# Moving the gather of an expert's sixth pair of rows from the third fixed unit to the first unit behind the branch

## The chip, the cores and the metric

The kernel runs on one core of one Trainium2 chip. The metric is the device time of one execution in microseconds (us); lower is better. Before the change three runs took 1734.55 to 1735.56 us, median 1735.2. The engines are called PE (TensorE, matrix products), ACT (ScalarE), DVE (VectorE), POOL (GpSimd) and SP (SyncE, which issues transfers). Each works through its own queue of instructions in order and waits for the others by semaphores.

## The reference

An attention without softmax makes the rows, then a mixture of eight experts works on some of them:

```python
# u, v: (8, 2496, 256), z: (8, 2496, 64); x becomes (19968, 256)
scores = z @ z.T / 2496
x = u * (maximum(scores, 0) ** 2 @ v)
do_compute = x @ w_skip > 0            # the other rows pass unchanged
e = argmax(x @ w_gate)                 # one expert of 8 for each row, with its gate
y = gate * (maximum(x @ w1[e], 0) @ w2[e])    # w1: 256 x 1024, w2: 1024 x 256
out = x + y
```

With the reference's inputs (seed 0) 10,022 of the 19,968 rows go to an expert: 1191, 1245, 1235, 1194, 1290, 1073, 1292 and 1502 to experts 0 to 7.

## The kernel before

The attention fills the first 1245 us or so. It writes the rows x to a DRAM tensor `xr` and, as each block of rows is routed, each row's number and gate to a list `lst` of its expert. Matrix products run in fp32r with a high and a low part, three products for one (`w1h`, `w1l`, `xh`, `xl`, `hh`, `hl`).

The expert stage goes through the experts in order. A **pair** is 256 rows of one expert, two tiles of 128 rows. Before a pair can be used it is gathered by `fetch` (L633): DVE copies its 256 row numbers into a small tile `go` (L637), then POOL issues two indirect DMAs (L639), each of which brings 128 rows of 1 KB from `xr`. Then `turn_pe` (L649) transposes the rows: PE turns four 128 x 128 blocks (L657), ACT takes the high part out of PSUM (L659), DVE the low part (L660). Tiles of gathered rows are called `xgf` for pairs 0 to 2 and `xgu` for later ones.

`unit` (L662) does the work on up to 512 rows. Its parts are hidden blocks `h_part` (PE L691, ACT L696 for `hh`, DVE L697 for `hl`) and pieces of the second product `y_part` (PE L710). The parts follow each other in an order written out by hand, first `lead` hidden blocks, then hidden blocks and second products in turn. `fills` is a table from a slot number to steps: the steps in slot k are issued right behind part k, into the queues of their engines, in the order of the program. So with `lead` 4, slot 1 lies behind the second hidden block, slot 3 behind the fourth, and in a unit of 256 rows slot 5 behind the second piece of the second product. At the end of a unit DVE forms the output rows (L739) and POOL scatters them, 128 a DMA (L742).

Each expert has three **fixed units** of one pair each (NFIX = 3), whatever its count. Behind them stands a **branch** (`tc.Switch`, L1032): a register holds how many pieces of 64 rows are left (`arm`), and each engine jumps to the code written for that number. `widths` (L977) cuts the pieces into units of up to 8: 7 or 8 pieces make one unit, 9 make 4 + 5, 12 make 8 + 4. In the counts above experts 0 to 7 take the code for 7, 8, 8, 7, 9, 5, 9 and 12 pieces.

The branch needs pairs 3, 4 and, where more than 1280 rows go to the expert, 5. In the kernel before, all three are gathered ahead of the branch for every expert (L1000; for expert 0 L1014 and L1017), one in each fixed unit, for pair 5 in the third. Behind the branch, L1045 to L1047 gather pairs 6 and later if there are any, `there` being the last pair that has been asked for. Entries of a list past its count point to a spare row, so that a gather of rows that don't exist reads that row.

In the queues around this place: DVE makes the `go` copies between the `hl` blocks. POOL, for experts after the first, also makes the low parts of the next expert's weights (L153, L159), gathers the next expert's pairs (L1004) and scatters the outputs. In the third fixed unit POOL's order is: scatters of the second unit, gather of pair 5, four subtractions of weights, gather of the next expert's pair 2, scatters of the third unit, branch. SP loads the weights (L97) into four staging tiles, each of which is free again when its subtraction is done. Transfers that are issued inside a branch come with an instruction of POOL for their semaphores (INC_SWDGE_SEM).

Of the kernel before, what the change touches and what calls it, by code (L numbers as in the profile page):

```python
# [23 lines left out]
NFIX = 3  # L24
# [20 lines left out]
def f32(ap):  # L45
    return ap.bitcast(F32)
# [3 lines left out]
def attn_moe(ctx, tc, zT, uT, v, wg, w1, w2, cst, pad, out):  # L50
# [75 lines left out]
    def load_w(e, eng):  # L126

        w1h, w1l, w2t = wts[e] = ([], [], [])
        raw = {}
        srcs = []  # L130
        for k in range(4):
            c, h = divmod(k, 2)
            srcs.append(
                w1[e, c * P : (c + 1) * P, h * 2 * D : (h + 1) * 2 * D].rearrange("p (a d) -> p a d", a=2)
            )
        for k in range(NF // 2):
            srcs.append(w2[e, :, 2 * k : 2 * k + 2, :])
        ahead = 3

        def bring(k):  # L140
            for m in range(len(raw), min(k, len(srcs))):
                raw[m] = stage_in(srcs[m])

        bring(3)

        def piece(k):
            bring(k + ahead)
            r = raw[k]
            if k < 4:
                w1h.append(vtile("w1h"))  # L150
                w1l.append(vtile("w1l"))
                nc.scalar.copy(w1h[k], r)
                eng.tensor_sub(w1l[k], r, f32(w1h[k]))  # L153
            else:
                for a in range(2):
                    t = vtile("w2t")
                    w2t.append(t)
                    nc.scalar.copy(t[:, 0, :], r[:, a, :])
                    eng.tensor_sub(t[:, 1, :], r[:, a, :], f32(t[:, 0, :]))  # L159

        return [lambda k=k: piece(k) for k in range(len(srcs))]
# [262 lines left out]
    def spare(rows64=True):  # L424

        if rows64:
            return ps_s.tile([P, 2, QC], F32, name="psm", tag="s")
        return ps_acc.tile([P, 1, QC], F32, name="psm", tag="acc")
# [201 lines left out]
    def load_ids(t, e, n):  # L630
        nc.sync.dma_start(t, lst[e * CAP : e * CAP + n * P, :].rearrange("(k p) c -> p k c", p=P))

    def fetch(ids, xg, n=2):  # L633


        go = rp.tile([P, 2, 1], I32, name="go", tag="go", bufs=4)
        nc.vector.tensor_copy(go[:, :n], ids[:, :, 0:1])  # L637
        for t in range(n):
            nc.gpsimd.indirect_dma_start(  # L639
                out=xg[:, t, :],  # L640
                out_offset=None,
                in_=xr,
                in_offset=bass.IndirectOffsetOnAxis(ap=go[:, t, 0:1], axis=0),
                bounds_check=N + P - 1,
                oob_is_err=False,
            )
        return xg

    def turn_pe(xg, xt, n=2, o=0, rows64=False):  # L649

        if rows64:
            ps = spare()[:, 0, :].rearrange("p (d q) -> p d q", d=2)
        else:
            ps = ps_acc.tile([P, 2, 2 * P], F32, name="pst", tag="acc")
        for t in range(n):
            for d in range(2):
                nc.tensor.transpose(ps[:, d, t * P : (t + 1) * P], xg[:, t, d * P : (d + 1) * P], ident)  # L657
        xh, xl = (x[:, :, o : o + n * P] for x in xt)
        nc.scalar.copy(xh, ps[:, :, : n * P])  # L659
        nc.vector.tensor_sub(xl, ps[:, :, : n * P], f32(xh))  # L660
# [193 lines left out]
    for s, (ci, p) in enumerate(steps):  # L854
        b, q0, n = chunks[ci]
        k = s % NP
# [110 lines left out]
    def ids_of(e, i, n=2):  # L967
        return idts[e][:, 2 * i : 2 * i + n, :]

    def pair(e, i):  # L970

        return xgs["f"][NFIX * (e % 2) + i] if i < NFIX else xgs["u"][i % 4]

    def turned(e, i):
        return xtf if e and i == 0 else xts[i % 2]
# [9 lines left out]
    def add(fills, *slots):  # L985
        for k, f in slots:
            fills.setdefault(k, []).append(f)

    def rows(e, i):
        return lambda: fetch(ids_of(e, i), pair(e, i))  # L990

    for e in range(E):
        more = e + 1 < E
        wq = load_w(e + 1, nc.gpsimd if e else nc.vector) if more else []
        narms = NARM + (2 if e == 0 else 1)
        for i in range(NFIX):
            fills = {}
            if e:

                add(fills, (1, rows(e, i + 3)), (3, lambda: turn_pe(pair(e, i + 1), turned(e, i + 1))))  # L1000
                if e == 1 and i == 0:
                    add(fills, (0, rows(1, 2)))
                if more:
                    add(fills, (4, rows(e + 1, i)))  # L1004
                if i == 0 and e + 2 < E:
                    add(fills, (6, lambda: load_ids(idts[e + 2], e + 2, 2 * NSTAT)))
                add(fills, *zip((1, 3, 5), wq[3 * i : 3 * i + 3]))
            elif i == 0:
                add(fills, (0, lambda: turn_pe(pair(0, 1), turned(0, 1))))
                add(fills, (1, gates), (1, logits), (1, route), (2, counts), (2, gate), (2, rows0), (2, rows1),  # L1010
                    (2, store), (4, store), (5, end_routes), (6, end_lists))
                add(fills, *zip((0, 2), left))
            elif i == 1:
                add(fills, (1, end_counts), (3, lambda: turn_pe(pair(0, 2), turned(0, 2))), (4, rows(0, 3)), (6, rows(0, 4)))  # L1014
                add(fills, *zip((1, 3, 5), wq[:3]))
            else:
                add(fills, (1, rows(1, 0)), (3, rows(0, 5)), (4, lambda: turn_pe(pair(0, 3), turned(0, 3))),  # L1017
                    (5, rows(1, 1)), (6, lambda: load_ids(idts[2], 2, 2 * NSTAT)))
                add(fills, *zip((1, 2, 3, 5, 6), wq[3:]))
            if more and i == NFIX - 1:  # L1020
                add(fills, (7, lambda: turn_pe(pair(e + 1, 0), turned(e + 1, 0))))
            if i == NFIX - 1:

                add(fills, (5, lambda: turn_pe(pair(e, NFIX + 1), turned(e, NFIX), 2, 2 * P)))
                n = nc.values_load(fin["arm"][0:1, e : e + 1], min_val=0, max_val=narms - 1)
                add(fills, (1, lambda: tc.switch_hint({g: n for g in ENGINES}, narms, label="rest%d" % e)))
            ids = ids_of(e, i) if e else idt_e[:, 2 * i : 2 * i + 2, :]
            xg = pair(e, i)
            unit(e, 4, ids, [xg[:, 0, :], xg[:, 1, :]], turned(e, i), fills)


        for arm in tc.Switch(n, narms, hint="rest%d" % e):  # L1032
            ws = widths(arm) if arm <= NARM else []
            if arm > NARM:
                for i in range(NFIX):
                    xg = fetch(ids_of(0, i), xgs["u"][i])
                    turn_pe(xg, xts[0])
                    unit(0, 4, ids_of(0, i), [xg[:, 0, :], xg[:, 1, :]], xts[0])
            end = NFIX + -(-sum(ws) // 4)
            i, there = NFIX, NFIX + 2  # L1040
            for j, hw in enumerate(ws):
                fills = {}
                after = ws[j + 1 :]
                nxt = i + -(-hw // 4)
                while there < min(i + 3, end - 1):  # L1045
                    there += 1
                    add(fills, (1, rows(e, there)))  # L1047
                if after:
                    xt = xts[(NFIX + j + 1) % 2]
                    add(fills, (3, lambda nxt=nxt, xt=xt: turn_pe(pair(e, nxt), xt)))  # L1050
                    if after[0] > 4:
                        add(fills, (5, lambda nxt=nxt, xt=xt: turn_pe(pair(e, nxt + 1), xt, 2, 2 * P)))
                w = -(-hw // 2)
                xg = [pair(e, i + t // 2)[:, t % 2, :] for t in range(w)]
                unit(e, hw, ids_of(e, i, w), xg, xts[(NFIX + j) % 2], fills, not more and not after, 3 if j else 4)
                i = nxt
            if arm >= NARM:
                ce = nc.values_load(fin["cnt"][0:1, e : e + 1], min_val=0, max_val=N)
                with tc.For_i((NSTAT if arm == NARM else NFIX) * UT, ce, UT) as tok:
                    it = op.tile([P, 2, 2], I32, name="it", tag="it")  # L1060
                    nc.sync.dma_start(
                        it, lst[bass.ds(tok + e * CAP, UT), :].rearrange("(k p) c -> p k c", p=P)
                    )
                    xg = fetch(it, xgs["u"][0])
                    turn_pe(xg, xts[0])
                    unit(e, 4, it, [xg[:, 0, :], xg[:, 1, :]], xts[0])
# [55 lines left out]
```

## Time and profile before

| | |
|---|---|
| median of three runs | 1735.2 us |
| the profiled execution's own time | 1747.1 us |
| its span, first to last instruction | 1745.1 us |
| mean granted clock of TensorE | 0.996 |
| busy: PE, DVE, ACT, POOL | 99%, 69%, 64%, 30% |
| expert stage | about 1245 to 1745 us |
| HBM read, written | 184.2 MB, 136.0 MB |

A row of the time line reads: start in us, length in us, engine, line of the kernel, operation, tiles as out<-in, shape, count, and in brackets the idle time of the engine before it with what ended it. A row of the groups reads: line, engine, operation, tiles, shape, count, then busy us and mean ns, then idle time before and what ended most of it. A row of the waits reads: who waited for whom, us in total, times, the longest. A row of stretches gives start:end, length, busy us (and instructions) of PE, PEld (weight loads), DVE, ACT and POOL, then the granted clock, the busy share of the 16 DMA engines and GB/s. "issue" stands for time in which an engine waited for nothing that the profile shows.

### The profile page before, as it was taken

The page shows a single profiled execution, that of the slowest core. Times are in us where ns is not written, and L with a number is a line of the kernel's source. Part 1 is how long each engine was busy: PE and PEld are TensorE (multiplying, and loading weights), DVE is VectorE, ACT ScalarE, POOL GpSimd, SP SyncE. Part 2 cuts the span into 40 slices and gives each one's busy share as a digit, 9 for nine tenths or more (in the row PEclk, how much of TensorE's full clock was granted, in tenths as well). Part 3 has the DMA queues.
Part 4 walks back from the last instruction along what each step waited for, and adds up shares of the span by engine and source line. Part 5 has one row for each costly group of instructions (what it writes and reads, how often), then busy time and mean ns, then how long its engine had stood idle before and what let it go on. Part 6 is the DMA issues. An engine that isn't in the chain of part 4 may idle for free.

```text
span 1745.1 us, 39255 instructions
## 1 busy us (share of the span) xinstructions
PE 1724.1 (99%) x15474; PEld 1537.9 (88%) x15474; DVE 1206.2 (69%) x1976; ACT 1112.6 (64%) x1409; POOL 520.1 (30%) x516
## 2 busy tenths in 40 slices
PE   9999999999999999999999999999989999999998
PEld 7888789988888998888889888888889999999997
DVE  6877877887887888788788878877744334443333
ACT  7877877787687778768777876877333333333321
POOL 1103213212211321231132023112446556635731
PEclk9999999999999999999999999999999999999999
DMA  5576699579858957985895799589543323322210
GB/s 179 152 203 193 151 247 281 144 211 258 236 146 243 277 147 204 272 239 146 236 262 162 207 261 254 140 225 250 149 111 84 90 83 106 100 61 86 86 42 26
DMA packets 408113, 303.29 MB, mean 174 GB/s; under 512 B 202768, under 2 KB 346001, under 8 KB 407152
## 3 DMA queue, kind: packets, MB, share of 16 engines
q1 hardware_dynamic: 393728, 276.37, 57.6%
q0 software_dynamic: 13632, 22.99, 4.7%
q8 instruction: 137, 2.24, 0.5%
q14 instruction: 184, 1.51, 0.3%
q10 hardware_dynamic: 432, 0.18, 0.0%
HBM read 184.21 MB, written 136.02 MB: 183 GB/s over the span
## 4 chain that ended last, share of the span: by engine, by line
PE 90%; DMA 3%; issue 3%; DVE 1%; ACT 1%; another core or an unknown queue 1%; POOL 1%; SPq 0%; POOLq 0%; DVEq 0%; ACTq 0%
PE acc L419 59%; PE y L710 10%; PE psh L691 10%; PE ps L302 8%; DMA out<-o,idt 2%; PE psm L491 1%; PE pst L657 1%; PE ps L285 0%; DMA kept<-rt 0%; DVE hl L697 0%; DVE al L390 0%; DMA raw<-in_v 0%; ACT ah L386 0%; DMA xgu<-xr,go 0%
## 5 line engine op out<-in xcount | busy, mean ns | idle before, releaser
L419 PE MATMUL acc<-ah,vh 64*128 64x512 f32 (+1 forms) x3120 | 643.7, 384 | 0.9 <-DVE ah L386 0.8
L419 PE MATMUL acc<-ah,vl 64*128 64x512 f32 (+1 forms) x3120 | 629.4, 383 | 0.0
L390 DVE TENSOR_TENSOR al<-r,ah 128x1024 fp32r<-128x1024 f32 (+1 forms) x400 | 479.8, 1206 | 135.2 <-ACT ah L386 114.9
L419 PE MATMUL acc<-al,vh 64*128 64x512 f32 (+1 forms) x3120 | 499.0, 383 | 0.6 <-DVE al L390 0.2
L590 POOL DMA_INDIRECT lst<-pair,dest x160 | 202.4, 1265 | 773.5 <-DVE dest L588 688.7
L386 ACT CAST ah<-r 128x1024 fp32r<-128x1024 f32 (+1 forms) x356 | 363.5, 1032 | 90.4 <-PE acc L419 41.8
L419 PEld LDWEIGHTS acc<-ah,vh 64*128 64x128 f32 x3120 | 329.3, 185 | 48.1 <-DVE ah L386 1.6
L419 PEld LDWEIGHTS acc<-ah,vl 64*128 64x128 f32 x3120 | 329.6, 185 | 41.6 <-DVE vl L122 0.3
L419 PEld LDWEIGHTS acc<-al,vh 64*128 64x128 f32 x3120 | 312.5, 184 | 51.0 <-DVE al L390 7.7
L376 ACT ACTIVATE r<-ps 128x1024 f32<-128x1024 f32 (+1 forms) x224 | 228.0, 1018 | 134.6 <-PE ps L302 116.1
L696 ACT ACTIVATE hh<-psh 128x512 fp32r<-128x512 f32 (+2 forms) x172 | 96.3, 572 | 287.6 <-PE psh L691 233.1
L377 ACT ACTIVATE r<-r 128x1024 f32<-128x1024 f32 (+1 forms) x224 | 236.3, 1055 | 7.1
L710 PE MATMUL y<-w2t,hh 128*128 128x256 f32 (+1 forms) x1328 | 235.8, 280 | 0.0
L697 DVE SCALAR_TENSOR_TENSOR hl<-psh,hh 128x512 fp32r<-128x512 f32 (+2 forms) x172 | 110.0, 655 | 151.9 <-ACT hh L696 121.3
L319 DVE STREAM_TRANSPOSE rt<-r 128x512 f32<-128x512 f32 x304 | 197.4, 688 | 10.2 <-DMA kept<-rt 9.4
L710 PEld LDWEIGHTS y<-w2t,hh 128*128 128x128 f32 (+1 forms) x1328 | 201.1, 186 | 1.8 <-issue 0.6
L691 PE MATMUL psh<-xt,w1h 128*128 128x256 f32 (+3 forms) x896 | 185.8, 304 | 8.6 <-DVE hl L697 5.9
L710 PE MATMUL y<-w2t,hl 128*128 128x256 f32 (+1 forms) x664 | 184.8, 278 | 0.8 <-DVE hl L697 0.7
L691 PEld LDWEIGHTS psh<-xt,w1h 128*128 128x128 f32 x896 | 142.4, 190 | 14.5 <-DVE hl L697 7.3
L691 PE MATMUL psh<-xt,w1l 128*128 128x256 f32 (+3 forms) x448 | 135.3, 302 | 0.0
L742 POOL DMA_INDIRECT out<-o,idt x77 | 76.5, 994 | 167.6 <-DVE o L739 132.5
L710 PEld LDWEIGHTS y<-w2t,hl 128*128 128x128 f32 (+1 forms) x664 | 123.0, 185 | 1.2 <-DVE hl L697 1.2
(197 smaller groups left out, 1750.6 us busy)
## 6 DMA issues: line engine op xcount, KB each, us to landing
kept<-rt SPq DMA_DIRECT2D x242, 256.0 KB
r<-kept SPq DMA_DIRECT2D x90, 512.0 KB
r<-kept SPq DMA_DIRECT2D x62, 448.0 KB
raw<-in_v SPq DMA_DIRECT2D x80, 256.0 KB
ut<-in_uT SPq DMA_DIRECT2D x32, 512.0 KB
xr<-xrow SPq DMA_DIRECT2D x128, 128.0 KB
out<-xr SPq DMA_DIRECT2D x32, 512.0 KB
raw<-in_w SPq DMA_DIRECT2D x64, 256.0 KB
```

The costliest lines, as they stand in the source:

```text
L302: nc.tensor.matmul(to, k[h, o : o + P], queries(ci, q, h, n), start=(m == 0), stop=(m == 2))
L319: nc.vector.transpose(t[:, :, 32 * k : 32 * k + 32].rearrange("p (k a) i -> p a k i", k=4), r[:, x, :].rearrange("p (a k i) -> p a k i", a ...
L376: nc.scalar.activation(r[:, :, :n], ps[:, :, :n], AF.Relu, scale=isc)
L377: nc.scalar.activation(r[:, :, :n], r[:, :, :n], AF.Square)
L386: (nc.scalar.copy if on_act(ci, p) else nc.vector.tensor_copy)(h_, r_)
L390: nc.vector.tensor_sub(l_, r_, f32(h_))
L419: nc.tensor.matmul(acc[t][:, :n], w[h, x, dd], a[h, x, :n], start=(first and t not in halves[:m]), stop=(last and t not in halves[m + 1 :]),)
L590: put = nc.gpsimd.indirect_dma_start(out=lst, out_offset=bass.IndirectOffsetOnAxis(ap=dest[:, t : t + 1], axis=0), in_=pair[:, t, :], in_o ...
L691: nc.tensor.matmul(ps[:, j * W : (j + 1) * W], wt[:, a, o : o + P], x[:, d, :W], start=(m == 0), stop=(m == 5),)
L696: nc.scalar.activation(hh[:, : G * W], ps[:, : G * W], AF.Relu)
L697: nc.vector.scalar_tensor_tensor(hl[:, : G * W], ps[:, : G * W], 0.0, f32(hh[:, : G * W]), op0=ALU.max, op1=ALU.subtract)
L710: nc.tensor.matmul(ys[t], h[:, tt], w2t[f][:, k, :], start=(f == 0 and m == 0 and t % share == 0), stop=(f == NF - 1 and m == 2), skip_gro ...
```

## The change

The gather of pair 5 leaves the third fixed unit, for expert 0 as for the others. Behind the branch the count of pairs already asked for now begins at 4. The first unit there gathers in slot 1 the first pair that is missing and in slot 3 the second, if there is one. So pair 5 is gathered in slot 1 of the first unit behind the branch, by the same three instructions, and only in the code for 9 pieces and more (those that reach pair 5).

```diff
-                add(fills, (1, rows(e, i + 3)), (3, lambda: turn_pe(pair(e, i + 1), turned(e, i + 1))))
+                if i < NFIX - 1:
+                    add(fills, (1, rows(e, i + 3)))
+                add(fills, (3, lambda: turn_pe(pair(e, i + 1), turned(e, i + 1))))
...
-                add(fills, (1, rows(1, 0)), (3, rows(0, 5)), (4, lambda: turn_pe(pair(0, 3), turned(0, 3))),
+                add(fills, (1, rows(1, 0)), (4, lambda: turn_pe(pair(0, 3), turned(0, 3))),
...
-            i, there = NFIX, NFIX + 2
+            i, there = NFIX, NFIX + 1
...
-                while there < min(i + 3, end - 1):
-                    there += 1
-                    add(fills, (1, rows(e, there)))
+                for k in range(1, min(i + 3, end - 1) - there + 1):
+                    add(fills, (1 + 2 * (k > 1), rows(e, there + k)))
+                there = max(there, min(i + 3, end - 1))
```

## The prediction

> **What bounds the kernel now.** I read the page first, then the waits of TensorE (PE) from the start of the expert stage at 1240 us, then the rows around the eight branches.
>
> ```profile
> PE 1724.1 (99%) x15474; PEld 1537.9 (88%) x15474; DVE 1206.2 (69%) x1976; ACT 1112.6 (64%) x1409; POOL 520.1 (30%) x516
> ```
> ```profile
> PE psh L691 <- DVE hl L697: 5.9, 4, 2.8
> PE psh L691 <- issue: 2.6, 4, 0.9
> PE y L710 <- DVE hl L697: 0.7, 1, 0.7
> PE psm L564 <- DVE pre L546: 0.5, 1, 0.5
> ```
>
> PE is the bound, and in the 505 us of the expert stage it waits 5.9 + 2.6 + 0.7 + 0.5 = 9.7 us. So whatever this change saves on another engine is worth at most a part of 9.7 us, while any wait that it puts in front of PE costs its full length. The four waits of 5.9 us all lie just behind a branch. The two longest are those of experts 0 and 5, the other two together are 5.9 - 2.78 - 1.90 = 1.2 us (experts 1 and 3):
>
> ```profile
> 1297.69 0.47 PE L691 MATMUL psh<-xt,w1h 128*128 128x448 f32 x1 [2.78 <-DVE hl L697]
> ```
> ```profile
> 1592.46 0.56 PE L691 MATMUL psh<-xt,w1h 128*128 128x320 f32 x2 [1.90 <-DVE hl L697]
> ```
>
> No PE wait on a gather stands in the list: every pair of rows is there in time today.
>
> **Which experts need a sixth pair.** With the reference's inputs (seed 0) the experts get 1191, 1245, 1235, 1194, 1290, 1073, 1292 and 1502 tokens. Behind the 768 of the three fixed units that leaves 7, 8, 8, 7, 9, 5, 9, 12 pieces of 64, which the code cuts into units of 7; 8; 8; 7; 4+5; 5; 4+5; 8+4. The trace agrees, at 32 such matmuls a unit (8 blocks of F, 2 halves of D, 2 terms):
>
> ```profile
> L691 PE MATMUL psh<-xt,w1h 128*128 128x512 f32 x96 | 30.5, 399 | 1.0 <-DVE hl L697 0.6 <-issue 0.4
> ...
> L691 PE MATMUL psh<-xt,w1h 128*128 128x320 f32 x96 | 22.1, 317 | 1.9 <-DVE hl L697 1.9
> ...
> L691 PE MATMUL psh<-xt,w1h 128*128 128x448 f32 x64 | 18.6, 371 | 3.9 <-DVE hl L697 3.4 <-issue 0.5
> ```
>
> Three units of 8 pieces, three of 5, two of 7. Only experts 4, 6 and 7 reach pair 5. So the change drops the gather in experts 0, 1, 2, 3 and 5, and moves it in three.
>
> **What is removed.** Per expert one index copy on DVE and two indirect gathers on POOL:
>
> ```profile
> L639 POOL DMA_INDIRECT xgu<-xr,go x48: 997/1016/1256, 1272.0 to 1698.8; - x48
> L637 DVE COPY go<-idt x45: 154/159/2807, 1271.5 to 1696.3; 128x2 int32<-128x2 int32 x45
> ```
> ```profile
> 1686.21 1.05 POOL L639 DMA_INDIRECT xgu<-xr,go  x1 [2.23 <-DVE go L637]
> 1687.56 1.01 POOL L639 DMA_INDIRECT xgu<-xr,go  x1 [0.30 <-issue]
> ```
>
> On POOL that is 2 x (1.02 + 0.30) = 2.6 us per expert ahead of the branch. What stood behind it there moves up by 2.6 us: four subtractions of the next expert's weights, the two gathers of its pair 2, and, as far as the results are ready, two scatters. PE waits for none of these, so as POOL time the 2.6 us are worth nothing; the 0.16 us on DVE neither, in a unit where PE does not wait for DVE. What could be worth something is traffic. DVE sits idle at each branch; these stretches run from its last output row to its first instruction behind the branch, in experts 1, 5, 6 and 7 (the columns I use are the length and, next to last, the DMA share):
>
> ```profile
> 1351.71:1354.99 3.28, 3.28 (x15) 2.44 (x13) 0.00 (x1) 1.69 (x3) 2.95 (x5) 1.00 0.71 229
> 1589.17:1591.92 2.75, 1.39 (x10) 1.13 (x8) 0.01 (x2) 0.95 (x3) 2.14 (x3) 1.00 0.73 209
> 1644.06:1645.92 1.86, 1.86 (x18) 1.86 (x18) 0.00 (x0) 0.92 (x2) 1.56 (x2) 1.00 0.15 35
> 1705.26:1706.63 1.37, 1.37 (x8) 1.09 (x7) 0.00 (x1) 0.60 (x1) 1.06 (x2) 1.00 0.01 6
> ```
>
> Busy DMA engines go with 2.8 to 3.3 us, idle ones with 1.4 to 1.9 us. Expert 6 gathers pair 5 like the others; what it lacks is the load of a next but one expert's weights. Those loads wait for the staging tiles that POOL's subtractions free. In experts 1 and 5 these are:
>
> ```profile
> 1353.22 2.81 POOL L159 TENSOR_TENSOR w2t<-raw,w2t 128x256 fp32r<-128x256 f32 x4
> ```
> ```profile
> 1585.54 2.81 POOL L159 TENSOR_TENSOR w2t<-raw,w2t 128x256 fp32r<-128x256 f32 x4
> ```
>
> In expert 5 they end at 1588.4, just ahead of the idle stretch, and would end at 1585.8, so that the loads run mostly before it (expert 3 lies alike); in expert 1 they would end at 1353.4, and the loads move into the stretch (expert 2 alike). I take -1.0 us for experts 3 and 5 together (2.75 - 1.86 = 0.9 in expert 5) and 0 for the rest. Bounds: -2.6 us (all of 1.2, the 0.43 us of expert 2 that is one of the "issue" waits, and 1.0 of expert 5's 1.90), and +1.0 us if experts 1 and 2 get later by 0.5 each.
>
> **What is added.** Behind the branch the gather is issued after the second hidden block (slot 1), and PE turns pair 5 in slot 5 of experts 4 and 6 and in slot 3 of expert 7. PE gets there today at:
>
> ```profile
> 1532.70 0.60 PE L657 MATMUL pst<-ident,xgu 128*128 128x128 f32 x4
> ```
> ```profile
> 1650.44 0.60 PE L657 MATMUL pst<-ident,xgu 128*128 128x128 f32 x4
> ```
> ```profile
> 1709.79 0.60 PE L657 MATMUL pst<-ident,xgu 128*128 128x128 f32 x4
> ```
>
> The second half of the pair is needed about 0.18 us later. When will it be there? The index copy stands on DVE behind the second `hl`:
>
> ```profile
> 1529.03 1.89 DVE L697 SCALAR_TENSOR_TENSOR hl<-psh,hh 128x512 fp32r<-128x512 f32 x3 [2.96 <-issue]
> ```
> ```profile
> 1645.92 1.89 DVE L697 SCALAR_TENSOR_TENSOR hl<-psh,hh 128x512 fp32r<-128x512 f32 x3 [1.87 <-ACT hh L696]
> ```
> ```profile
> 1706.63 0.69 DVE L697 SCALAR_TENSOR_TENSOR hl<-psh,hh 128x512 fp32r<-128x512 f32 x1 [1.37 <-ACT hh L696]
> 1707.87 0.69 DVE L697 SCALAR_TENSOR_TENSOR hl<-psh,hh 128x512 fp32r<-128x512 f32 x1 [0.54 <-issue]
> ```
>
> Three in 1.89 us are 0.60 apart, so the second ends at 1530.3, 1647.2 and 1708.6, and the copy 0.16 later. From the copy's end to the first gather this trace has 0.28 us (1282.63 + 0.16 to 1283.07) and 0.79 us (1685.26 + 0.16 to 1686.21, the row above):
>
> ```profile
> 1282.63 0.16 DVE L637 COPY go<-idt 128x2 int32<-128x2 int32 x1
> ...
> 1283.07 1.24 POOL L639 DMA_INDIRECT xgf<-xr,go  x1 [3.27 <-DVE go L637]
> ```
> ```profile
> 1685.26 0.16 DVE L637 COPY go<-idt 128x2 int32<-128x2 int32 x1
> ```
>
> The second gather starts 1.35 us after the first (above), or 1.42 us as two transfers do inside a branch:
>
> ```profile
> 1529.58 1.00 POOL L742 DMA_INDIRECT out<-o,idt  x1 [0.31 <-issue]
> 1536.84 0.98 POOL L742 DMA_INDIRECT out<-o,idt  x1 [6.25 <-DVE o L739]
> 1538.26 0.97 POOL L742 DMA_INDIRECT out<-o,idt  x1 [0.45 <-DVE hl L697]
> ```
>
> Landing is seen where two gathers run alone, those of 1686.21 and 1687.56; the DMA engines are busy with them in these two stretches and idle between them:
>
> ```profile
> 1687.90:1688.70 0.80, 0.80 (x10) 0.80 (x9) 0.40 (x1) 0.00 (x0) 0.68 (x1) 1.00 0.66 184
> 1689.20:1690.50 1.30, 1.30 (x14) 1.30 (x14) 0.00 (x0) 0.00 (x0) 0.00 (x0) 1.00 0.37 101
> ```
>
> So 2.5 and 2.9 us from a gather's start to its last packet. From the end of the second `hl` it is 0.16 + (0.28 to 0.79) + (1.35 to 1.42) + (2.5 to 2.9) = 4.3 to 5.3 us until all has landed:
> - expert 7: landed 1712.9 to 1713.9, wanted 1710.0: a stall of 2.9 to 3.9 us, I take 3.3;
> - expert 4: 1534.6 to 1535.6, wanted 1532.9: 1.7 to 2.7 us. Should DVE come 1.1 us earlier (2.96 to expert 6's 1.86), it is 0.6 to 1.6. I take 1.6, the middle of 0.6 and 2.7;
> - expert 6: 1651.5 to 1652.5, wanted 1650.6: 0.9 to 1.9 us, I take 1.3.
>
> POOL must have left the branch too. In expert 4 its last scatter of the fixed unit ends at 1530.6 today (1529.58 + 1.00) and 2.6 us earlier then, before the copy at 1530.5. The wait stands in PE's queue ahead of the rest of the second product (experts 4 and 6) or of the fifth hidden block (7); ACT and DVE have only the turned pair to do, so nothing covers it and nothing gives it back. Sum of the added waits: 3.3 + 1.6 + 1.3 = 6.2 us, bounds 2.9 + 0.6 + 0.9 = 4.4 and 3.9 + 2.7 + 1.9 = 8.5.
>
> The Trainium skill, "DMA: Bandwidth & Descriptors", section "Anatomy of one DMA — SWDGE (gpsimd) path", fits a POOL transfer with 2.0 us plus its bytes over 436 GB/s; for the 128 KB here that is 2.3 us as an estimate, where the trace has 2.5 to 2.9. By it each stall would be about 0.4 us shorter and the sum 5.0 instead of 6.2 us; the measured landing decides.
>
> **The sum.** 6.2 - 1.0 = +5.2 us. The profiled execution took 1747.1 us (span 1745.1), 0.7% over the median of 1735.2; on 5 us that is nothing, so the forecast is 1735.2 + 5.2 = 1740.4 us. A measurement of this kernel can tell about 0.2%, 3.5 us, from no change: the limits are 1731.7 and 1738.7.
>
> **The rivals.**
> - Only expert 7 pays. If DVE and POOL are through the branch a microsecond or two earlier in experts 4 and 6, their gathers land in time: 3.3 - 1.0 = +2.3, 1737.5 us. For it: slot 5 lies 3.3 us behind slot 3. Against: expert 6 has idle DMA engines at its branch already and still comes out late. 0.14.
> - All three hidden, 1735.2 - 1.0 = 1734.2 us. It needs the 4.3 us above to be under 1.4 in expert 7. 0.05.
> - Relief at the branch, the other side. If the dropped gathers' traffic is what keeps DVE idle there, the stretches shrink to expert 7's 1.37 us everywhere and the PE waits of 2.78, 1.90, 1.2 and 0.43 us go, 6.3 us; the copies come 1.6 and 0.5 us earlier in experts 4 and 6, which leaves stalls of about 0.6 and 0.8 us. With expert 7's 3.3 us that is -6.3 + 4.7 = -1.6, 1733.6 us (0.05). Where POOL and DVE, so relieved, also bring the three gathers in time, it is -6.3, 1728.9 us (0.04). It decides from a DMA share of 0.15 or less in those stretches. Against: the weight loads remain, and expert 6 has the gather and a share of 0.15 all the same. The Trainium skill, "DMA: Bandwidth & Descriptors", section "Latency and other measured facts", lets the fixed cost of a transfer fall with a lighter load on the memory, which speaks for this rival; the four stretches agree in direction.
> - POOL is the late one. Its branch bookkeeping, or code that comes after DVE's, holds the first gather back another microsecond in each of the three experts: 6.2 + 3.0 - 1.0 = +8.2, 1743.4 us. For it: in expert 7 POOL's first instruction behind the branch is at 1708.3, only 0.4 us before the copy ends, and its semaphore bookkeeping there takes 0.27 to 1.42 us apiece:
>
> ```profile
> L1032 POOLq BRANCH_PREFETCH_HINT  x8: 40/46/47, 1299.1 to 1708.3; - x8
> ```
> ```profile
> L1118 POOLq INC_SWDGE_SEM  x35: 274/863/1420, 1299.3 to 1737.4; - x35
> ```
>
> I give it 0.14.
>
> **How the numbers follow.** The forecast has 0.58. Slower by over 0.2%: 0.58 + 0.14 = 0.72. Within 0.2%: 0.14 + 0.05 + 0.05 = 0.24. Faster: 0.04. The forecast's own bounds are 4.4 - 2.6 = +1.8 and 8.5 + 1.0 = +9.5, 1737.0 to 1744.7; with the small cases on the low side, and cut where all three worst ends would have to meet, I give 1735.0 to 1744.0.
>
> **What would show it.** In the changed kernel: 38 gathers named xgu instead of 48; new PE waits before L657 on a DMA, about 3.3 us at expert 7 and 1 to 2 us at experts 4 and 6; POOL's subtractions ahead of the branch 2.6 us earlier; DVE's idle at the branch within 0.5 us of now in experts 1 and 2 and shorter by up to 0.9 in 3 and 5. I am wrong if expert 7 shows no such wait, or if PE's waits behind the branch change by more than 2.6 us.

## The result and the profile after

| | before | after |
|---|---|---|
| median, same chip (4 runs each) | 1735.4 us | 1754.7 us (1751.8 to 1756.6) |
| ratio after / before, 95% interval | | 1.011 (1.0095 to 1.0124) |
| the profiled execution's own time, its span | 1747.1, 1745.1 us | 1753.9, 1752.0 us |
| mean granted clock of TensorE | 0.996 | 0.992 |

The change costs 19.4 us, where 5.2 were forecast with a range up to +8.8: the sign was right, the size far off. The profiled execution of before reached expert 0's branch 8.6 us later than that of after: PE's first matmul behind it starts at 1289.81 against 1281.22 us. That lies in the part ahead of the branches and differs from execution to execution (the same changed kernel, profiled again, is there at 1287.46). So only what follows that matmul is compared. From it to the end the two executions take 455.3 and 470.8 us, +15.5 us. About 4 of the 19.4 us between the medians are thus not in this pair of traces; a second measurement of both kernels, below, gave +14.6.

The first view is the busy line of the page of after. PE is the bound as before, POOL has 10 instructions fewer (506 against 516).

```profile
PE 1725.2 (98%) x15474; PEld 1537.4 (88%) x15474; DVE 1205.3 (69%) x1971; ACT 1112.6 (64%) x1409; POOL 510.0 (29%) x506
```

Second, PE's waits from 1240 us on in after (us in total, times, the longest). Before had four rows with 9.7 us, none of them on a gather. Now 12.5 us are on the gather of pair 5, and of the old waits 2.3 are left.

```profile
PE pst L657 <- DMA xgu<-xr,go: 12.5, 6, 3.6
PE psh L691 <- DVE hl L697: 2.3, 2, 1.7
```

Third, the time line of PE in after at the six waits. The two in expert 4 sum to 3.1 us, in expert 6 to 4.1, in expert 7 to 5.3.

```profile
1522.02 0.41 PE L657 MATMUL pst<-ident,xgu 128*128 128x128 f32 x2 [2.09 <-DMA xgu<-xr,go]
...
1523.46 0.44 PE L657 MATMUL pst<-ident,xgu 128*128 128x128 f32 x2 [1.03 <-DMA xgu<-xr,go]
...
1643.43 0.41 PE L657 MATMUL pst<-ident,xgu 128*128 128x128 f32 x2 [2.45 <-DMA xgu<-xr,go]
...
1645.51 0.69 PE L657 MATMUL pst<-ident,xgu 128*128 128x128 f32 x2 [1.67 <-DMA xgu<-xr,go]
...
1710.72 0.44 PE L657 MATMUL pst<-ident,xgu 128*128 128x128 f32 x2 [3.60 <-DMA xgu<-xr,go]
1712.84 0.69 PE L657 MATMUL pst<-ident,xgu 128*128 128x128 f32 x2 [1.69 <-DMA xgu<-xr,go]
```

Fourth, stretches cut at the moment where DVE reaches each branch, for experts 4, 5, 6, 7 and the end from DVE's last row on. Behind the length stand the busy time of PE, PEld, DVE, ACT and POOL, and then the granted clock. Before:

```profile
1525.00:1588.10 63.10, 63.10 (x532) 63.10 (x532) 25.84 (x49) 21.15 (x43) 34.14 (x36) 1.00 0.30 84
1588.10:1643.00 54.90, 53.00 (x434) 52.73 (x433) 19.41 (x41) 17.46 (x37) 31.45 (x33) 0.97 0.27 82
1643.00:1704.60 61.60, 61.60 (x519) 61.55 (x519) 24.08 (x46) 16.11 (x30) 19.92 (x21) 1.00 0.14 43
1704.60:1738.40 33.80, 33.59 (x243) 31.23 (x242) 11.97 (x21) 7.67 (x13) 6.75 (x7) 1.00 0.07 26
1738.40:1745.10 6.70, 0.00 (x0) 0.00 (x0) 0.31 (x1) 0.00 (x0) 1.13 (x2) 0.64 0.12 39
```

After:

```profile
1512.10:1580.20 68.10, 64.97 (x533) 64.57 (x532) 25.46 (x49) 21.13 (x43) 33.87 (x35) 0.97 0.27 75
1580.20:1633.20 53.00, 51.30 (x433) 51.04 (x432) 20.90 (x40) 17.45 (x37) 29.56 (x32) 1.00 0.22 71
1633.20:1701.80 68.60, 64.48 (x522) 64.03 (x521) 24.21 (x46) 15.95 (x30) 17.69 (x18) 0.95 0.13 38
1701.80:1744.00 42.20, 36.74 (x243) 33.53 (x241) 11.98 (x22) 7.77 (x13) 8.75 (x9) 0.92 0.08 27
1744.00:1752.00 8.00, 0.00 (x0) 0.00 (x0) 0.35 (x1) 0.00 (x0) 1.16 (x2) 0.63 0.09 33
```

Experts 4, 6 and 7 take 5.0, 7.0 and 8.4 us longer, the end 1.3. Expert 5 takes 1.9 less. Cut in the same way, experts 0 to 3 take 57.1, 58.0, 57.8 and 56.6 us after 57.5, 58.6, 58.5 and 57.3, together 2.4 less. All these stretches sum to +17.4 us, 1.9 more than the 15.5 above, because PE is further ahead of DVE at the first cut of before (1293.1 against 1289.81) than at that of after (1282.6 against 1281.22).

The waits are 12.5 us. The clock column has the next part: 0.97, 0.95 and 0.92 of full speed in the three experts that wait. A closer look at expert 7 in after, from ahead of the wait to behind it, shows how:

```profile
1700.00:1706.00 6.00, 6.00 (x34) 5.13 (x33) 2.21 (x5) 1.39 (x3) 1.94 (x2) 1.00 0.15 52
1706.00:1710.70 4.70, 1.12 (x5) 0.56 (x3) 1.55 (x4) 1.00 (x2) 1.90 (x2) 1.00 0.10 30
1710.70:1713.00 2.30, 0.59 (x3) 0.36 (x4) 0.00 (x0) 0.00 (x0) 0.15 (x1) 0.79 0.21 57
1713.00:1716.40 3.40, 3.40 (x11) 2.82 (x12) 0.69 (x1) 0.81 (x2) 0.00 (x0) 0.50 0.00 0
1716.40:1719.00 2.60, 2.60 (x13) 2.51 (x13) 0.69 (x1) 0.37 (x1) 0.00 (x0) 0.53 0.00 0
1719.00:1722.00 3.00, 3.00 (x21) 2.70 (x20) 0.69 (x1) 0.60 (x1) 0.00 (x0) 1.00 0.00 0
```

PE is idle for most of the time from 1707.1 to 1712.8. From about 1712.0, still in its second wait, to 1718.8 it is granted half its clock, although from 1712.8 on it is busy throughout, and after that the full clock again. The rows count 24 matmuls in the 6.0 us of half clock and 21 in the 3.0 us behind them. Half clock comes in periods of about 3.4 us, and each costs half of what PE works in it, at most 1.7 us: one such period in expert 4, two each in experts 6 and 7, as 68.10 x 0.03, 68.60 x 0.05 and 42.20 x 0.08 also say within the rounding. In experts 6 and 7 they begin while PE still waits, for 1.7 us (1643.75 to 1645.5) and 0.8 us of their 6.8, and there half clock costs nothing. So the three lose 1.7, 2.6 and 3.0, 7.3 us. With the waits that gives 4.8, 6.7 and 8.3 us, where the stretches are 5.0, 7.0 and 8.4 longer. Before had one period, in expert 5 (0.97), that is gone now.

The account from PE's first matmul behind the first branch on has four terms. The waits on the gather are 12.5 us and the half clock behind them 7.3. The end is 1.3 longer. The relief is -5.7: in before, PE's idle stretches just behind the branches are 2.78, 0.57, 0.43, 0.64 and 1.90 us in experts 0, 1, 2, 3 and 5, 6.3 us, and in after 0.60 and 1.70 in experts 0 and 5, 4.0 less, and the 1.7 us of expert 5's half clock are gone. Together that is 15.4 us, where 15.5 were measured.

The Trainium skill, "TensorE: Matmul & The Clock Gate", section "Part 1: The HAM clock gate", has a gate with just these two speeds, closed by an idle window of about 3.4 us and opened by one of busy work. The 0.50 and the 3.4 us agree with the trace. Its rule in the section "HAM oscillation — how this bites in real kernels", no idle gaps over about 3.4 us, does not tell these traces' cases apart: expert 4's gaps of 2.09 and 1.03 us with work between them were followed by half clock too, and so was before's 1.90 us in expert 5, while before's 2.78 us in expert 0 were not. In before the clock (third column from the end) is 1.00 behind expert 0's wait and 0.50 behind expert 5's:

```profile
1297.70:1301.10 3.40, 3.40 (x22) 3.26 (x23) 2.15 (x4) 0.55 (x1) 0.00 (x0) 1.00 0.05 19
...
1593.50:1596.90 3.40, 3.40 (x17) 3.40 (x16) 0.59 (x2) 0.44 (x1) 0.00 (x0) 0.50 0.12 41
```

Why is the gather so late? POOL in after at expert 7, behind it POOL's semaphore instructions in that stretch (nanoseconds: shortest/median/longest, then the first and last start), and DVE:

```profile
1703.61 0.97 POOL L742 DMA_INDIRECT out<-o,idt  x1 [0.30 <-issue]
1707.85 1.05 POOL L639 DMA_INDIRECT xgu<-xr,go  x1 [3.27 <-DVE hl L697]
1709.84 1.01 POOL L639 DMA_INDIRECT xgu<-xr,go  x1 [0.95 <-issue]
```
```profile
L1120 POOLq INC_SWDGE_SEM  x3: 1424/1441/1492, 1705.6 to 1709.7; - x3
```
```profile
1704.80 1.29 DVE L697 SCALAR_TENSOR_TENSOR hl<-psh,hh 128x512 fp32r<-128x512 f32 x2 [2.36 <-issue]
1706.01 0.16 DVE L637 COPY go<-idt 128x2 int32<-128x2 int32 x1
```

The index copy ends at 1706.17, the first gather starts 1.68 us later and the second 1.99 us after that. DVE is named as the releaser, but its `hl` was done at 1706.09. What lies between is POOL's own: it enters the branch's code and runs a first INC_SWDGE_SEM from 1705.6 to 1707.1, and another begins 0.15 us ahead of each gather. Those of expert 7 take 1.42 to 1.49 us. Experts 4 and 6 are alike: there the first gather starts 1.55 and 1.95 us behind the copy (0.78 and 1.28 us of them the first INC_SWDGE_SEM's length), and the second follows after 1.35 and 1.79 us.

The landing differs too. The DMA engines move these two gathers alone in all three experts; expert 4's two, one of expert 6 and one of expert 7 are seen here (the last column is GB/s):

```profile
1520.00:1523.10 3.10, 0.41 (x2) 0.20 (x2) 0.00 (x0) 0.00 (x0) 0.63 (x1) 1.00 0.40 85
...
1641.50:1643.10 1.60, 0.00 (x0) 0.00 (x0) 0.00 (x0) 0.00 (x0) 1.01 (x1) 1.00 0.34 82
...
1711.50:1712.50 1.00, 0.00 (x0) 0.00 (x0) 0.00 (x0) 0.00 (x0) 0.00 (x0) 0.76 0.49 131
```

The same 128 KB are moved within 1.6 us in expert 6 and within 1.0 in expert 7. Of the 256 rows of pair 5, experts 4 and 6 have 10 and 12 (1290 and 1292 less 1280), and all other entries read the one spare row; expert 7 has 222. That reading one row again and again is what makes them slower would fit, but no run tried it.

### The profile page after: what moved, and what is told of

Same layout as the page of the kernel before. It is cut to its first block, busy times and chain, and to the rows that moved or that the text cites. A ratio compares the mean times of both kernels' runs of the same rounds, so it can differ in the third digit from the quotient of the medians.

```text
span 1752.0 us, 39227 instructions
## 1 busy us (share of the span) xinstructions
PE 1725.2 (98%) x15474; PEld 1537.4 (88%) x15474; DVE 1205.3 (69%) x1971; ACT 1112.6 (64%) x1409; POOL 510.0 (29%) x506
## 5 line engine op out<-in xcount | busy, mean ns | idle before, releaser
L710 PE MATMUL y<-w2t,hh 128*128 128x256 f32 (+1 forms) x1328 | 239.6, 283 | 0.0
L710 PEld LDWEIGHTS y<-w2t,hh 128*128 128x128 f32 (+1 forms) x1328 | 204.6, 189 | 1.4
L710 PE MATMUL y<-w2t,hl 128*128 128x256 f32 (+1 forms) x664 | 186.5, 281 | 0.0
L710 PEld LDWEIGHTS y<-w2t,hl 128*128 128x128 f32 (+1 forms) x664 | 125.0, 188 | 0.0
```

The source lines that it names most:

```text
L710: nc.tensor.matmul(ys[t], h[:, tt], w2t[f][:, k, :], start=(f == 0 and m == 0 and t % share == 0), stop=(f == NF - 1 and m == 2), skip_gro ...
```

## The experiments

The kernel before ran beside each set on the same chip: 1739.4 us (17 runs) beside the first four, 1742.7 (24 runs) beside the last four. Chips differ by some us, so ratios are within a set. Where a time from PE's first matmul behind the first branch to the end is given, it stands against 455.3 us of before and 470.8 of after.

**The relief alone.** The gather of pair 5 is dropped in experts 0, 1, 2, 3 and 5 and stays ahead of the branch in 4, 6 and 7. This is right for these counts only. Against the changed kernel:

```diff
-                if i < NFIX - 1:
+                if i < NFIX - 1 or e in (4, 6, 7):
...
-            i, there = NFIX, NFIX + 1
+            i, there = NFIX, NFIX + (2 if e in (4, 6, 7) else 1)
```

> Experts 4, 6 and 7 gather pair 5 in the third fixed unit as before; experts 0, 1, 2, 3 and 5 no longer gather it there (their code behind the branch does, if it is reached). Theory (the loss is made in the three experts that use pair 5, by PE's wait for the gather and the half clock after it; the other five gain 4.2 us in the two traces): 1735.4 - 4.2 = 1731 us, no PE wait on xgu, PE clock 1.0 through the expert stage. Rival (the loss is bookkeeping that a gather in the code of a branch costs every expert, reached or not): 1735 to 1741 us.

It took 1735.6 us, 0.9981 (0.997 to 0.9991) of before, -3.8 us. PE's waits of this kernel from 1240 us on:

```profile
PE psh L691 <- DVE hl L697: 1.5, 2, 1.2
PE psh L691 <- PE pst L657: 0.4, 1, 0.4
```

The 1735.6 us lie in the rival's absolute range, but on this chip before took 1739.4, and the -3.8 us are what the theory gave (-4.2), where the rival had 0 or more. No wait on a gather and no half clock. From the first matmul behind the branch on it takes 450.8 us, 4.5 less than before, although the end is 1.8 longer. Expert 5 takes 52.4 us, near after's 53.0; the end takes 8.5 us, near after's 8.0. So dropping gathers is a gain, and all the loss comes from the three that move. That every expert pays for bookkeeping behind its branch is refuted.

**The move alone.** The other half: moved in experts 4, 6 and 7, kept ahead of the branch in the rest.

```diff
-                if i < NFIX - 1:
+                if i < NFIX - 1 or e not in (4, 6, 7):
...
+                add(fills, (1, rows(1, 0)), (3, rows(0, 5)), (4, lambda: turn_pe(pair(0, 3), turned(0, 3))),
...
-            i, there = NFIX, NFIX + 1
+            i, there = NFIX, NFIX + (1 if e in (4, 6, 7) else 2)
```

> Experts 4, 6 and 7 gather pair 5 behind the branch; the other five as in the kernel before. Theory: the change without its relief, 1754.7 + 4.2 = 1759 us, with PE waits on xgu of about 3, 4 and 5 us in experts 4, 6 and 7 and the clock at 0.5 for some us after each. Rival (bookkeeping in every expert): below the change, 1745 to 1752 us.

It took 1756.5 us, 1.0099 (1.0079 to 1.012), +17.1 us, and 471.4 us from the first matmul behind the branch on, 0.6 more than after and not the 4.2 more that were expected. The five other experts do lose after's relief (expert 5 has a wait of 1.94 us and half clock behind it, as in before), but expert 7 and the end are shorter than in after. Expert 7's PE waits, POOL gathers and semaphore instructions:

```profile
1716.51 0.44 PE L657 MATMUL pst<-ident,xgu 128*128 128x128 f32 x2 [2.56 <-DMA xgu<-xr,go]
1718.00 0.44 PE L657 MATMUL pst<-ident,xgu 128*128 128x128 f32 x2 [1.05 <-DMA xgu<-xr,go]
```
```profile
1713.59 1.05 POOL L639 DMA_INDIRECT xgu<-xr,go  x1 [2.18 <-DVE go L637]
1714.95 1.02 POOL L639 DMA_INDIRECT xgu<-xr,go  x1 [0.30 <-issue]
```
```profile
L1120 POOLq INC_SWDGE_SEM  x3: 258/266/309, 1712.5 to 1714.3; - x3
```

The code for 12 pieces is the same, yet here the semaphore instructions take 0.3 us instead of 1.4 to 1.5, the second gather follows the first by 1.36 us instead of 1.99, and PE waits 3.6 us instead of 5.3 and loses one period of half clock instead of two. In both kernels the first gather starts 0.6 + 0.15 us behind the end of the first INC_SWDGE_SEM (1705.6 + 1.49 + 0.75 = 1707.84; 1712.5 + 0.31 + 0.75 = 1713.56), and the pace between the two is that instruction's length plus about 0.6 us, unless this is under 1.36. Expert 6 of after fits with a length of 1.22: 1.8 us, and expert 4 with 0.72: 1.35 us. Experts 4 and 6 wait 3.1 and 4.2 us here, as in after.

**Keeping PE's clock.** The changed kernel with idle matmuls of `ones` with `ones` ahead of pair 5's transposes, so that PE works while it would wait. They are 50 in expert 4, 66 in expert 6 and 88 in expert 7; what is computed stays.

```diff
+    def busy(n):
+        pj = ps_acc.tile([P, 1, QC], F32, name="psj", tag="acc")
+        for _ in range(n):
+            nc.tensor.matmul(pj[:, 0, :P], ones, ones, start=True, stop=True)
...
+                    if e in (4, 6, 7) and nxt == 5:
+                        add(fills, (3, lambda: busy(88)))
...
+                        if e in (4, 6, 7) and nxt + 1 == 5:
+                            add(fills, (5, lambda: busy({4: 50, 6: 66, 7: 66}[e])))
```

> The change, with idle matmuls (ones by ones, never read) ahead of the transposes of pair 5: 50, 66 and 88 in experts 4, 6 and 7, about 3, 4 and 5 us, so that PE works where it waited. Theory (after a wait of some us the array runs at half clock for some us, which costs 8 us over the three): the waits are filled, the clock stays at 1.0, 1754.7 - 8 = 1747 us. Rival (only the wait itself costs, and the slow rows behind it are a matter of recording or of another cause): 1754 to 1757 us.

It took 1750.1 us, 1.0064 (1.0044 to 1.0084); the changed kernel in the other set has 1.0079 (1.0062 to 1.0097), so the medians of the two sets do not part them, and the traces must. From the first matmul behind the branch on it takes 464.5 us, 6.3 less than after. PE's waits and the stretches around the three waiting places:

```profile
PE pst L657 <- DMA xgu<-xr,go: 2.1, 3, 0.9
```
```profile
1507.00:1535.00 28.00, 27.43 (x256) 27.16 (x255) 11.07 (x21) 7.71 (x17) 12.63 (x14) 1.00 0.30 88
1626.00:1654.00 28.00, 27.06 (x262) 26.79 (x261) 10.20 (x20) 7.11 (x15) 13.06 (x14) 1.00 0.18 52
1699.00:1722.00 23.00, 22.36 (x191) 19.77 (x190) 6.64 (x12) 5.38 (x9) 4.01 (x4) 1.00 0.08 26
```

The clock stays at 1.00 in all three. The half clock was thus a cost of its own behind the waits, and idle work takes it away. Not all 7.3 us come back: the idle matmuls take 11.9 us, and 2.1 us of waiting remain, together 1.5 us more than the 12.5 they stand for.

**An earlier index copy.** The gather behind the branch is put into slot 0 instead of slot 1, one hidden block earlier.

```diff
-                    add(fills, (1 + 2 * (k > 1), rows(e, there + k)))
+                    add(fills, (3 * (k > 1), rows(e, there + k)))
```

> The change with the gather behind the branch issued in slot 0 instead of slot 1, one hidden block (1.4 us of PE) earlier. Theory (POOL is what is late: from its entry behind the branch it first works through its own semaphore instruction of 1.4 to 1.5 us, and the index copy is done long before): the gathers start at most 0.3 us earlier in each expert, 1753 to 1755 us. Rival (the prediction's own step: the copy behind the second hl on DVE sets the start): 0.6 to 1.4 us earlier in each of the three, 1749 to 1752 us.

It took 1753.0 us, 1.0082 (1.0061 to 1.0103). DVE and POOL of this kernel in expert 7, and its PE waits:

```profile
1705.32 0.69 DVE L697 SCALAR_TENSOR_TENSOR hl<-psh,hh 128x512 fp32r<-128x512 f32 x1 [2.38 <-issue]
1705.93 0.16 DVE L637 COPY go<-idt 128x2 int32<-128x2 int32 x1
```
```profile
1708.27 1.04 POOL L639 DMA_INDIRECT xgu<-xr,go  x1 [3.19 <-DVE hl L697]
1710.26 1.02 POOL L639 DMA_INDIRECT xgu<-xr,go  x1 [0.95 <-issue]
```
```profile
PE pst L657 <- DMA xgu<-xr,go: 12.6, 6, 3.6
```

The copy now starts 0.6 us after the first `hl`, where in after it was 1.2, and the gather starts 2.2 us behind the copy's end (1708.27 less 1706.09) instead of 1.7. The waits are the same 12.6 us as the 12.5 of after. What sets the start of the gather is POOL, not DVE and not the copy: in all three experts it comes 0.75 to 0.85 us behind the end of the first INC_SWDGE_SEM. The time could not have told this. It is 13.6 us over before in its set, which the rival also allows, and the changed kernel itself was measured at 19.4 and 14.6 us over before.

**The changed kernel again,** beside the three kernels that follow.

> The changed kernel itself once more, so that it stands beside the other runs on one chip. All theories: 19 us (1.1%) over the kernel before, with PE waits on xgu of 3.1, 4.1 and 5.3 us; the half clock behind them may be one period of 3.4 us more or less.

It took 1757.3 us, 1.0079 (1.0062 to 1.0097). That is 14.6 us over before in this set, not the 19 expected. The waits are 3.4, 3.7 and 5.6 us, the half clock has the same five periods, and from the first matmul behind the branch on it takes 470.1 us (470.8 in after). So the expert stage cost the same, close to 15 us more than in before, and the rest of the first measurement's 19.4 was not seen again.

**A later need.** The gather stays as changed, but PE turns pair 5 later: slot 9 instead of 3 in the unit of 8 pieces, slot 6 instead of 5 in that of 4.

```diff
-                    add(fills, (3, lambda nxt=nxt, xt=xt: turn_pe(pair(e, nxt), xt)))
+                    add(fills, (9 if hw == 8 else 3, lambda nxt=nxt, xt=xt: turn_pe(pair(e, nxt), xt)))
...
-                        add(fills, (5, lambda nxt=nxt, xt=xt: turn_pe(pair(e, nxt + 1), xt, 2, 2 * P)))
+                        add(fills, (6, lambda nxt=nxt, xt=xt: turn_pe(pair(e, nxt + 1), xt, 2, 2 * P)))
```

> The change with pair 5 turned later: in expert 7 in slot 9 of the first unit instead of slot 3 (about 8 us of PE work later), in experts 4 and 6 in slot 6, its end, instead of slot 5 (2.7 us later). Theory (all is PE's wait and the half clock it brings): expert 7's wait of 5.3 us and its 3.4 us of half clock are gone, 8.5 us; in experts 4 and 6 the wait on the gather is shorter by 2.7 us but the conversion of the turned rows (0.6 on ACT, 0.7 on DVE) now stands open, so 1 to 4 us less in both together: 10 to 12 us under the change, 1.004 of the kernel before. Rival (the time lies elsewhere in the branch's code, its fetch or its bookkeeping): within 3 us of the change.

It took 1744.5 us, 1.0011 (1.0002 to 1.0021), 12.8 us less than the changed kernel in the same set. Its PE waits that concern pair 5, and the turn in expert 7:

```profile
PE pst L657 <- DMA xgu<-xr,go: 2.2, 2, 1.6
...
PE psh L691 <- ACT xt L659: 1.4, 2, 0.7
```
```profile
1711.78 0.60 PE L657 MATMUL pst<-ident,xgu 128*128 128x128 f32 x4
```

In expert 7 the turn waits for nothing. Experts 4 and 6 have only one slot to give: 2.2 us of waiting remain, and the hidden block right behind the turn now waits for ACT to take the high part out. No half clock is left, and from the first matmul behind the branch on it takes 455.3 us, as much as before. So nearly the whole loss is the lateness of the gather against its need, and the clock that PE loses with it; what remains eats up the relief that the dropped gathers bring.

**Is the relief POOL's time?** The first experiment again, with eight clears of pair 5's tile on POOL in place of each dropped gather. They take 2.1 us together, near the 2.6 of the two gathers, and move no data.

```diff
+    def idle_pool(e):
+        for k in range(8):
+            nc.gpsimd.memset(pair(e, 5)[:, k % 2, :], 0.0)
...
+                else:
+                    add(fills, (1, lambda: idle_pool(e)))
```

> The first experiment (pair 5 gathered ahead of the branch in experts 4, 6 and 7 only), with eight clears of 0.3 us on POOL in the place of each dropped gather: POOL is as busy as before, DMA engines are not. On the relief of 3.8 us: if it is POOL's time and the earlier weight loads, it is gone, 1.000 of the kernel before; if it is the traffic of the dropped gathers, it stays, 0.998.

It took 1738.2 us, 0.9977 (0.9965 to 0.999), and 451.2 us from the first matmul behind the branch on against 450.8 of the first experiment. The relief stays with POOL nearly as busy as before. It is not POOL's time.

**A later place ahead of the branch.** The kernel before with one edit: pair 5 is gathered in slot 6 of the third fixed unit instead of slot 1 (slot 3 for expert 0). No expert's gather is dropped or moved behind the branch, so it is right for any counts. Against the kernel before:

```diff
-                add(fills, (1, rows(e, i + 3)), (3, lambda: turn_pe(pair(e, i + 1), turned(e, i + 1))))
+                add(fills, (6 if i == NFIX - 1 else 1, rows(e, i + 3)), (3, lambda: turn_pe(pair(e, i + 1), turned(e, i + 1))))
...
-                add(fills, (1, rows(1, 0)), (3, rows(0, 5)), (4, lambda: turn_pe(pair(0, 3), turned(0, 3))),
+                add(fills, (1, rows(1, 0)), (6, rows(0, 5)), (4, lambda: turn_pe(pair(0, 3), turned(0, 3))),
```

> The kernel before with pair 5 gathered in slot 6 of the third fixed unit instead of slot 1 (expert 0: slot 3), behind POOL's subtractions and the next expert's gather, for every expert. If the relief is POOL's time ahead of the weight loads, this has most of it with no dropped gather: 0.998; if it is the traffic, 1.000. Pair 5 is wanted some 8 us later and lands in about 5, so no wait on it or one under 1 us in expert 4.

It took 1737.7 us, 0.9972 (0.9958 to 0.9985), 5.1 us less than before in the same set. It beats both kernels. Its largest PE waits from 1240 us on:

```profile
PE psh L691 <- issue: 3.1, 3, 1.6
PE y L710 <- issue: 1.5, 2, 0.9
```

Experts 4 and 6 wait for no gather, though two idle stretches of PE, 0.60 and 0.85 us on L710, lie in them a little ahead of the turn, for a reason that the profile doesn't show. From the first matmul behind the branch on it takes 449.9 us, as little as with the gathers dropped. So the relief does not need fewer gathers, only that this one does not stand in slot 1 of the third fixed unit (slot 3 for expert 0). What about it costs time there, its traffic (which for experts 0, 1, 2, 3 and 5 is the spare row alone) or its index copy between DVE's `hl` blocks, was not tried separately and stays open.

## Why the prediction was wrong in size

**Right.** PE was and is the bound, only experts 4, 6 and 7 reach pair 5, and the new waits stand where they were put, the longest in expert 7; that expert 6 waits longer than expert 4 was not foreseen. As POOL time the dropped gathers are worth nothing. The relief has the sign forecast.

**The failed step: when the pair will be there.** The prediction took 0.28 to 0.79 us from the copy to the first gather, 1.35 to 1.42 to the second and 2.5 to 2.9 to land, and summed the waits to 6.2 (4.4 to 8.5). The start measured 1.55, 1.95 and 1.68 us in experts 4, 6 and 7, the second gather came 1.35, 1.79 and 1.99 us later, PE started 3.8, 4.0 and 3.0 us behind it, and the waits sum to 12.5. The start is the term that was too small in all three. The rows for it had been taken from code outside a branch, and the pace from scatters with short semaphore instructions. Behind the branch POOL's gathers go by its INC_SWDGE_SEM: the same code with 0.3 us instead of 1.4 apiece waits 3.6 us in expert 7, inside the predicted 2.9 to 3.9. The landing was measured to the last packet of gathers of 256 real rows; PE starts about 0.4 us behind it, and the gathers of experts 4 and 6, nearly all spare row, take longer to move, though nothing else runs beside them.

By the figure of the Trainium skill, "DMA: Bandwidth & Descriptors", section "Anatomy of one DMA — SWDGE (gpsimd) path", the landing would have been 2.3 us, as an estimate; measured were 2.9 to 4.0 from the gather's start to PE's, so it erred the same way as the forecast and further.

**The missing term.** The sum counted a wait at its length. PE's clock halves behind it, 7.3 us more in three experts, of which before's single period in expert 5 had been a sign: the 1.90 us wait there was followed by 3.4 us of half clock, 1.7 us lost, which the prediction did not look for. With idle matmuls in the waits the clock stayed at 1.00, and 6.3 us came back.

**The relief** was put at -1.0 us for experts 3 and 5 and at nothing for 0, 1 and 2. It is -5.7, in all five: 2.2 in expert 0, 0.57, 0.43 and 0.64 in experts 1 to 3, and 1.9 in expert 5 with its half clock. PE's waits behind the branches changed by 4.0 us, beyond the 2.6 that the prediction itself had named as a sign of being wrong. DVE's idle at the branch in after, experts 1 and 5 (length first), against 3.28 and 2.75 before:

```profile
1340.83:1343.46 2.63, 2.63 (x13) 2.10 (x12) 0.00 (x1) 1.20 (x3) 2.17 (x3) 1.00 0.83 280
...
1581.31:1583.86 2.55, 1.39 (x10) 1.13 (x8) 0.01 (x2) 0.93 (x3) 1.92 (x2) 1.00 0.32 102
```

Expert 1's stretch shrinks by 0.65 us although the DMA engines are busier in it (0.83 after 0.71), and expert 5's by only 0.2 although they are less so (0.32 after 0.73). These two rows contradict the reading that the DMA share sets this idle time.

**The end** was not in the sum: +1.3 us, because the last scatter starts 3.6 us behind DVE's last row (1744.4), where in before it was 0.3 us. Its semaphore instruction of 1.5 us is over at 1744.59; what POOL then waits for until 1747.74 the profile doesn't show. POOL's last row of after:

```profile
1747.95 0.97 POOL L742 DMA_INDIRECT out<-o,idt  x1 [3.76 <-POOLq L1034]
```

**The rivals.** "POOL is the late one" had the right mechanism, and the row of 0.27 to 1.42 us that it quoted was the right row; but it priced it at one extra microsecond an expert on the start alone, without the pace of the second gather and the clock. The rivals in which the gathers come in time are refuted by the 12.5 us. The relief at the branch, the rival on the other side, is larger than the sum had it (4.0 of the 6.3 us of waits went, and 1.7 us of half clock with them). That the traffic makes it is not shown, and 5.7 us are little beside the 12.5 + 7.3 of waits and clock.

## What to carry to other kernels

Before a transfer is moved behind a branch, look up how long its issuing engine's semaphore instructions take there, at their longest, and add the entry into the branch; durations from straight code are too short. A wait of about 2 us or more on TensorE can bring half clock behind it, up to 1.7 us a period here, so price it with that as an upper end, and where a wait can't be avoided, put the need later or fill it. And before a step is taken out of a critical neighbourhood, try it a few slots later on the same side: here that gave the whole gain (1737.7 against 1742.7 us) with no wait on the gather.

## What the runs showed of the hardware

INC_SWDGE_SEM does not have one length. It grows by 0.2 to 0.3 us from expert to expert and then falls back: in after 0.72 us in expert 4, 1.22 in 6 and 1.44 in 7; with the move alone 0.83, 1.34 and then 0.27. In expert 7 it was 0.3 us in the three kernels that keep the gather of pair 5 ahead of the branch in experts 0, 1, 2, 3 and 5 (before, the move alone, the later place) and 1.4 to 1.5 in those that drop it there (after, the relief alone, the one with clears), whether expert 7's own gather was moved or not. So it is not the code of the branch that sets it, but what was issued before; by what rule stays open.

The half clock came after 3.1 us of idle in two pieces and after 1.9 us in one (twice: before, and with the move alone), but not after waits of 1.2 to 1.7 us, nor after the 2.78 us in expert 0 of before. The length of a wait alone does not decide. Where half clock begins keeps to steps of 3.413 us: in after at 1524.29, 1643.75 and 1712.02, 35 and 20 steps apart. Counted back from 1593.51, where before's begins, expert 5's 1.90 us lie whole in one step (1590.10 to 1593.51), while expert 0's 2.78 us are cut into 1.64 and 1.14 by the step at 1296.55. That idle time counts within one such step fits these cases; how much of it is needed is not settled, since in expert 7 with the move alone 1.89 us in one step did not bring half clock and 1.73 us in the next one did.
